# First token tile's first column group in plain float32, and weight splits spread over later slots

## The chip, the cores and the metric

One core of a Trainium2 chip runs the whole program. The metric is the device time of one execution in microseconds; the profiled times come from one execution recorded by the hardware profiler. The engines are TensorE (PE in the rows; PEld is its weight load), VectorE (DVE), ScalarE (ACT), GpSimd (POOL) and SyncE (SP), which issues most DMAs. The engines run side by side, each its own instructions strictly in program order, and wait for one another by semaphores.

## What is computed

Three float32 stages follow one another: local attention with block summaries, a dense feed-forward layer with ELU, and a routed layer of eight experts.

```python
scores = concat(masked(scale * q @ k.T, |i-j| < 16), scale * q @ k_sum.T + log(32))
x   = softmax(scores) @ concat(v, v_sum)          # (1536, 512) after the heads are joined
h   = x @ w_in                                    # 512 -> 2048
g   = where(h > 0, h, exp(min(h, 0)) - 1)         # ELU
x2  = g @ w_out                                   # 2048 -> 512
# then top-1 routing of x2 over 8 experts, relu MLP 512 -> 1024 -> 512, times the gate
```

## The kernel before

Tokens go in four tiles of 384 (`t` = 0 to 3), the 2048 hidden columns in 16 slices of 128 (`f`), which form two column groups of eight. All instructions are placed by hand in a loop over slots `sl`; in the text a slot is also named by n = sl - 9. Group 0 goes through the token tiles 0 to 3 in n = 0 to 31, group 1 in the 32 slots behind.

**Attention.** Each head pair of a tile is two units `u`, and up to slot 17 one unit belongs to a slot: scores `pe_s` into PSUM (S), `dve_max`, `act_exp`, `norm` (a 3-element TENSOR_SCALAR and a reciprocal on VectorE, then the scaling of 360 columns on GpSimd, L287), a slot later the transposes `pe_t` (T), another slot later `act_t` and the output `pe_o` (O). From slot 18 two units are worked on per pair of slots: `pe_s2`, `pe_o2` and both `norm` in the even slot, both transposes in the odd one. Slots 0 to 7 also hold `busy` transposes of the identity, whose results nobody reads.

**Split operands.** The dense layer multiplies in a reduced format (fp32r) and keeps accuracy by splitting each operand in a high part (a ScalarE cast) and a low part (a subtract). For `x` that is `act_o` and `dve_o` (VectorE); for the weights `w_split` (ScalarE L381, GpSimd L382); for the ELU result `g_hi` (ScalarE L409) and `g_lo` (GpSimd L413). Each product is then three matmuls: high x high, high x low, low x high.

**Weights** arrive as 64-bit floats. `w_load` brings a slice of 512 KB into one of four raw buffers, `w_conv` makes float32 of it in three VectorE passes (L368, L372, L375), and `w_prefetch` starts the next load. `corder` says in which slot each slice is converted, `wpend` holds the converted slices whose split is due, and `split_next` takes one of them. Between slots 17 and 32 `w_stash` converts the slices of group 1 and writes them to DRAM.

**A dense slot** (n = 0 to 7) of tile 0 runs ahead: `mm1` of slice n + 2 (12 matmuls of 384 columns into one of two PSUM banks h), ELU of slice n (`elu_exp` on ScalarE, `elu_max` on VectorE, which frees the bank), `mm2` of slice n - 1 (9 matmuls of 512 columns into three banks acc). On TensorE the order is `pe_s`, `pe_o`, `mm2`, `mm1`, `pe_t`; on VectorE `dve_max`, `elu_max`, the conversions with `dve_o` and `norm` between them. Two splits are taken per slot. Slot 8 (n = -1) is written out by hand: it holds `mm1` of slices 0 and 1, the last fourth of each behind the last `pe_o` of tile 0.

**From n = 9** a slot is: ELU of the slice before, `g_hi`, `g_lo`, a split if one is pending, `prep_k` and `prep_va` in odd slots (among them the copies L197 and L198 on VectorE), `mm2` of two slices before, in even slots `pe_o2` and `pe_s2` with their VectorE work, `mm1`, and the `w_stash` conversion. `pe_s2` uses the S bank and one h bank, so it needs that bank's `elu_max`.

Buffers: W is a pool of 16 buffers, each with the high and the low half of one slice; `xT3` is the x buffer of token tile 3, which is first written in slot 26 (n = 17).

Of the kernel before, what the change touches and what calls it, by code (L numbers as in the profile page):

```python
# [9 lines left out]
F32 = mybir.dt.float32  # L10
# [39 lines left out]
def build(tc, cap, qT, kT, vT, vP, wi, wo, wg, wgT, wx, out):  # L50
# [6 lines left out]
    with ctx:  # L57
# [79 lines left out]
        xT = {}  # L137
        acc = {}
# [172 lines left out]
        def act_o(u):  # L311
            p, t, pr, g0 = where(u)
            if pr == 0 and g0 == 0:
                xT[t] = xpool.tile([P, 2, NCC, TT], F32R, tag=f"xT{t}", name=f"xT{t}")
            nc.scalar.copy(xT[t][:, 0, pr, g0 * QB : (g0 + GRP) * QB], PS["o", u][:, 0 : GRP * QB])

        def dve_o(u):
            p, t, pr, g0 = where(u)
            q = slice(g0 * QB, (g0 + GRP) * QB)
            nc.vector.tensor_tensor(  # L320
                xT[t][:, 1, pr, q], PS.pop(("o", u))[:, 0 : GRP * QB], xT[t][:, 0, pr, q].bitcast(F32),
                op=ALU.subtract)
# [35 lines left out]

        def w_conv(which, parts=(0, 1, 2)):
            for part in parts:  # L360
                for io, f in which:
                    if part == 0:
                        raw = RW[io, f]
                        t = mpool.tile([P, 512], U32, tag="t1", bufs=T1, name=f"t1{io}{f}")
                        RW[io, f] = (raw[:, :, 0], raw[:, :, 1], t)
                    lo, hi, t = RW[io, f]
                    if part == 0:
                        nc.vector.tensor_scalar(  # L368
                            out=t, in0=hi, scalar1=3, scalar2=0x3FFFFFF8,
                            op0=ALU.logical_shift_left, op1=ALU.bitwise_and)  # L370
                    elif part == 1:
                        nc.vector.scalar_tensor_tensor(  # L372
                            out=t, in0=hi, scalar=0xC0000000, in1=t, op0=ALU.bitwise_and, op1=ALU.bitwise_or)
                    else:
                        nc.vector.scalar_tensor_tensor(  # L375
                            out=t, in0=lo, scalar=29, in1=t, op0=ALU.logical_shift_right, op1=ALU.bitwise_or)
# [10 lines left out]
        def mm1(t, f, cs=range(NCC)):  # L387
            if cs[0] == 0:
                HP[t, f] = ph(f"h{t}_{f}")
            w = W["i", f]  # L390
            for c in cs:
                for n, (s, xs) in enumerate(((0, 0), (0, 1), (1, 0))):
                    nc.tensor.matmul(  # L393
                        HP[t, f][:, 0:TT], lhsT=w[:, s, c * P : (c + 1) * P], rhs=xT[t][:, xs, c, :],
                        start=c == 0 and n == 0, stop=c == NCC - 1 and n == 2)

        def elu_exp(t, f):
            e = EP[t, f] = mpool.tile([P, TT], F32, tag="e", name=f"e{t}_{f}")
            nc.scalar.activation(out=e, in_=HP[t, f][:, 0:TT], func=AF.Exp)  # L399
            nc.scalar.activation(out=e, in_=e, func=AF.Relu, bias=1.0, scale=-1.0)  # L400
# [6 lines left out]
        def g_hi(t, f):  # L407
            gT[t, f] = mpool.tile([P, 2, TT], F32R, tag="g", name=f"g{t}_{f}")
            nc.scalar.copy(gT[t, f][:, 0], EP[t, f])  # L409

        def g_lo(t, f, eng):
            g = gT[t, f]
            eng.tensor_tensor(g[:, 1], EP.pop((t, f)), g[:, 0].bitcast(F32), op=ALU.subtract)  # L413
# [3 lines left out]
        def mm2(t, f):  # L417
            gr = f // FPG
            w = W["o", f]
            g = gT.pop((t, f))  # L420
# [3 lines left out]
            for tb in range(BPT):  # L424
                for n, (s, ws) in enumerate(((0, 0), (0, 1), (1, 0))):
# [409 lines left out]
        for f in range(NFC):  # L835
            if f < FPG:
                corder.setdefault(LAG - 4 + f, []).append(("i", f))
                corder.setdefault(LAG - 1 + f - (f > 5), []).insert(0, ("o", f))
# [5 lines left out]
        nload = [0]  # L844

# [39 lines left out]
        for sl in range(total):  # L885
# [16 lines left out]
            cv = list(corder.get(sl, ())) if sl >= LAG else []  # L902

# [13 lines left out]
            if sl == LAG - 1:  # L917
# [4 lines left out]
                w_split("i", 2)  # L922
                pe_o(u - 2)
                act_o(u - 2)
                w_conv([("o", 0)], (0, 1))
                dve_o(u - 2)
                pe_t(u - 1)
                mm1(0, 1, range(NCC - 1))
                w_conv([("o", 0)], (2,))
# [3 lines left out]
                w_split("o", 0)  # L933
                w_conv([("i", 3)], (0, 1))
                act_o(u - 1)
                dve_o(u - 1)
                mm1(0, 0, range(NCC - 1, NCC))
                mm1(0, 1, range(NCC - 1, NCC))
                w_conv([("i", 3)], (2,))
                w_prefetch()  # L940
                wpend.append(("i", 3))
# [9 lines left out]
                g_hi(0, 0)  # L951
                g_lo(0, 0, nc.gpsimd)
# [183 lines left out]
            if dense:  # L1136
# [4 lines left out]
                split_next()  # L1141
# [10 lines left out]
                wpend.extend(cv)  # L1152
# [8 lines left out]
            if sl == LAG - 3:  # L1161
                w_conv([("i", 0)], (2,))
                w_prefetch()
                w_conv([("i", 1)], (0, 1))
            if sl == LAG - 2:
                w_conv([("i", 1)], (2,))
                w_prefetch()
# [4 lines left out]
            if sl in (LAG - 3, LAG - 2):  # L1172
                w_split("i", sl - LAG + 3)
            if sl == LAG - 2:
                w_conv([("i", 2)])
                w_prefetch()
            if sl == LAG - 4:
                w_conv([("i", 0)], (0, 1))
# [289 lines left out]
```

## Time and profile before

| | |
|---|---|
| median of 3 runs | 508.42 us (508.11 to 509.48) |
| the profiled execution | 508.64 us, of which 506.9 us is the span of its instructions |
| TensorE busy | 472.0 us, 93% |
| VectorE busy | 325.6 us, 64% |
| ScalarE busy | 271.8 us, 54% |
| GpSimd busy | 189.3 us, 37% |
| mean granted TensorE clock | 0.981 |

The shares are means over stages that differ, so the rows further down are taken by stretch. In a timeline row the first number is the start in us from the span's beginning, the second the time until the last of the merged instructions ended (the pipelined matmuls of neighbouring rows overlap a little), and the bracket tells for how long the engine stood idle before it and what ended that.

### The profile page before, as it was taken

To read this page: it belongs to the slowest core of one execution; us is meant where nothing else is said; L and a number is where in the kernel's file an instruction comes from. 1 tells how busy PE (TensorE), PEld (TensorE's weight loads), DVE (VectorE), ACT (ScalarE), POOL (GpSimd) and SP (SyncE) were. 2 spreads that over 40 slices of the span, in tenths; PEclk is the share of its full clock that TensorE was granted. 3 is DMA by queue.
4 is the path that set the end of the run, shared out by engine and by line. 5 is a ranking of instruction groups with operands and counts; after the bars stand their busy time and mean duration, and the time that the engine had idled before them with its cause. 6 is when DMAs were issued, how large, how long until landed. Compare 5 with 4: busy or idle time off the path is not lost.

```text
span 506.9 us, 9236 instructions
## 1 busy us (share of the span) xinstructions
PE 472.0 (93%) x3052; PEld 406.9 (80%) x3052; DVE 325.6 (64%) x880; ACT 271.8 (54%) x681; POOL 189.3 (37%) x197
## 2 busy tenths in 40 slices
PE   7798798889999999999999999999998999999892
PEld 6586577678888889999999899888767989888672
DVE  4699999878877761111149889846686755556460
ACT  4755656666667646664333333334654865566550
POOL 4345575633333335883223233223335040030440
PEclk9988998999999999999999999999999999999997
DMA  8996656667777441439010010012645966458380
GB/s 237 283 255 185 191 162 189 214 207 245 227 230 219 126 142 46 125 118 345 37 62 2 0 63 0 2 63 88 200 129 151 345 211 222 135 164 278 105 292 15
DMA packets 45634, 79.97 MB, mean 158 GB/s; under 512 B 4604, under 2 KB 19196, under 8 KB 45552
## 3 DMA queue, kind: packets, MB, share of 16 engines
q1 hardware_dynamic: 43792, 73.83, 46.4%
q0 software_dynamic: 1760, 5.19, 3.4%
q8 instruction: 34, 0.56, 0.5%
q14 instruction: 48, 0.39, 0.2%
HBM read 65.29 MB, written 13.11 MB: 155 GB/s over the span
## 4 chain that ended last, share of the span: by engine, by line
PE 65%; DVE 15%; DMA 13%; issue 2%; ACT 2%; POOL 1%; SPq 0%; DVEq 0%; POOLq 0%
PE acc L426 23%; PE h L393 22%; DMA xgq<-x2d,gidx 10%; PE bh L750 6%; PE y L739 5%; DMA vt<-vT 2%; DVE t1i L375 2%; DVE t1i L372 2%; DVE t1o L375 1%; DMA xg<-x2d,gidx 1%; PE T L294 1%; DVE st L285 1%; DVE sc L272 1%; PE O L334 1%; DVE t1o L372 1%
## 5 line engine op out<-in xcount | busy, mean ns | idle before, releaser
L393 PE MATMUL h<-xT,Wi 128*128 128x384 f32 x768 | 152.8, 346 | 8.2 <-DVE e L404 6.6
L393 PEld LDWEIGHTS h<-xT,Wi 128*128 128x128 f32 x768 | 137.2, 192 | 16.5 <-DVE e L404 8.7
L426 PE MATMUL acc<-Wo,g 128*128 128x512 f32 x576 | 145.8, 397 | 1.0 <-POOL Wo L382 1.0
L413 POOL TENSOR_TENSOR g<-e,g 128x384 fp32r<-128x384 f32 x63 | 71.4, 1133 | 145.5 <-ACT g L409 129.9
L426 PEld LDWEIGHTS acc<-Wo,g 128*128 128x128 f32 x576 | 105.9, 188 | 21.7 <-POOL Wo L382 1.3
L404 DVE SCALAR_TENSOR_TENSOR e<-e,h 128x384 f32<-128x384 f32 x64 | 35.3, 551 | 77.3 <-ACT e L400 77.3
L399 ACT ACTIVATE e<-h 128x384 f32<-128x384 f32 x64 | 31.4, 491 | 65.4 <-PE h L393 61.8
L409 ACT CAST g<-e 128x384 fp32r<-128x384 f32 x64 | 32.8, 513 | 42.6 <-DVE e L404 42.6
L618 DVE TENSOR_TENSOR E<-rawq,E 128x512 fp32r<-128x512 f32 x70 | 46.7, 705 | 9.1 <-ACT E L608 8.0
L279 ACT ACTIVATE sc<-sc,st 128x120 f32<-128x120 f32 x96 | 36.8, 385 | 28.8 <-DVE st L272 28.6
L750 PE MATMUL bh<-xbq,E 128*128 128x256 f32 (+1 forms) x288 | 43.6, 303 | 2.7 <-ACT ysf L654 1.4
L608 ACT CAST E<-rawq 128x512 fp32r<-128x512 f32 x75 | 42.7, 617 | 6.2 <-DMA rawq<-wx 3.5
L750 PEld LDWEIGHTS bh<-xbq,E 128*128 128x128 f32 x288 | 41.3, 188 | 5.0 <-ACT ysf L654 1.6
L287 POOL TENSOR_TENSOR sc<-sc,st 128x360 f32<-128x360 f32 x32 | 29.6, 925 | 41.3 <-DVE st L286 20.1
L739 PE MATMUL y<-E,g 128*128 128x512 f32 x168 | 41.7, 393 | 0.0
L488 DVE CUSTOM_DVE_ANT_0 dot<-a,wgb 128x512 f32<-128x512 f32 x48 | 40.0, 887 | 0.0
L739 PEld LDWEIGHTS y<-E,g 128*128 128x128 f32 x168 | 30.6, 188 | 5.7
L400 ACT ACTIVATE e<-e 128x384 f32<-128x384 f32 x64 | 33.7, 526 | 2.0
L272 DVE CUSTOM_DVE_ANT_0 sc<-S,masks 128x120 f32<-128x120 f32 x96 | 21.5, 276 | 14.2 <-PE S L247 10.4
L758 DVE TENSOR_TENSOR g<-e,g 128x256 fp32r<-128x256 f32 (+1 forms) x24 | 11.3, 469 | 23.8 <-ACT g L757 23.6
L655 POOL DMA_INDIRECT out<-ys,sidx x6 | 6.3, 1053 | 47.4 <-ACT ys L654 46.0
L755 ACT ACTIVATE e<-bh 128x256 f32<-128x256 f32 (+1 forms) x24 | 10.1, 419 | 22.4 <-PE bh L750 22.4
(225 smaller groups left out, 634.5 us busy)
## 6 DMA issues: line engine op xcount, KB each, us to landing
rawq<-wx SPq DMA_DIRECT2D x88, 256.0 KB, 4.3
rawi<-wi SPq DMA_DIRECT2D x16, 512.0 KB, 5.0
rawo<-wo SPq DMA_DIRECT2D x16, 512.0 KB, 5.5
vw<-vP SPq DMA_DIRECT2D x16, 288.0 KB, 6.7
kt<-kT SPq DMA_DIRECT2D x8, 400.0 KB, 5.6
qt<-qT SPq DMA_DIRECT2D x16, 192.0 KB, 5.9
vt<-vT SPq DMA_DIRECT2D x8, 384.0 KB
out<-xg SPq DMA_DIRECT2D x12, 256.0 KB, 3.6
```

What stands on the lines that cost most here:

```text
L279: nc.scalar.activation(out=sc[:, gi], in_=sc[:, gi], func=AF.Exp, bias=st[:, 0, gi : gi + 1], scale=-1.0, accum_out=st[:, 1, gi : gi + 1])
L393: nc.tensor.matmul(HP[t, f][:, 0:TT], lhsT=w[:, s, c * P : (c + 1) * P], rhs=xT[t][:, xs, c, :], start=c == 0 and n == 0, stop=c == NCC - ...
L400: nc.scalar.activation(out=e, in_=e, func=AF.Relu, bias=1.0, scale=-1.0)
L404: nc.vector.scalar_tensor_tensor(out=e, in0=e, scalar=-1.0, in1=h[:, 0:TT], op0=ALU.mult, op1=ALU.max)
L409: nc.scalar.copy(gT[t, f][:, 0], EP[t, f])
L413: eng.tensor_tensor(g[:, 1], EP.pop((t, f)), g[:, 0].bitcast(F32), op=ALU.subtract)
L426: nc.tensor.matmul(accp[tb], lhsT=g[:, s, tb * P : (tb + 1) * P], rhs=w[:, ws], start=f % FPG == 0 and n == 0, stop=f % FPG == FPG - 1 and ...
L488: nc.vector.tensor_tensor_reduce(out=junk, in0=x2[t * BPT + tb], in1=WGB[e // 2][:, e % 2], scale=1.0, scalar=0.0, op0=ALU.mult, op1=ALU.a ...
L608: (nc.vector.tensor_copy if m in vec else nc.scalar.copy)(EW[k][m][:, 0], raw_of(k, m))
L618: (nc.gpsimd if m in pool else nc.vector).tensor_tensor(w[:, 1], raw, w[:, 0].bitcast(F32), op=ALU.subtract)
L739: nc.tensor.matmul(ys[b], lhsT=g[:, s, b * P : (b + 1) * P], rhs=w[:, ws], start=f == 0 and n == 0, stop=f == 7 and n == 2)
L750: nc.tensor.matmul(h[:, 0:nt], lhsT=EW[k][half * NCC + c][:, ws, fc * P : (fc + 1) * P], rhs=xb[:, s, c, 0:nt], start=n == 0, stop=n == 3 ...
```

## The change

For token tile 0 and the eight slices of group 0, both products are computed with plain float32 operands: the converted weights and the unsplit `x` and ELU results, one matmul instruction in place of three. The unsplit weights stand in W buffers, two slices to a buffer (the last two, slices 6 and 7 of `w_out`, in half of the buffer that token tile 3's `x` takes later); the other half of that buffer holds the unsplit `x`. `dve_o`, `g_hi` and `g_lo` are left out there. The split parts are still needed: the weights' for the other token tiles, x's for group 1. The weights are split one slice per slot in n = 1 to 16, and `x` of tile 0 in n = 11 to 14 (`split_x0`). The conversions of group 0 move one or two slots later, so that slots n = 0 to 4 convert two slices and 5 to 7 one.

```diff
         def act_o(u):
             p, t, pr, g0 = where(u)
+            if t == 0:
+                if u == 0:
+                    x = xpool.tile([P, 2, NCC * TT], F32, tag=f"xT{NT - 1}", name="x0")
+                    X0.extend([x[:, 0].rearrange("p (c q) -> p c q", q=TT), x[:, 1].bitcast(U32)])
+                nc.scalar.copy(X0[0][:, pr, g0 * QB : (g0 + GRP) * QB], PS.pop(("o", u))[:, 0 : GRP * QB])
+                return
...
+        def split_x0(c):
+            if c == 0:
+                xT[0] = xpool.tile([P, 2, NCC, TT], F32R, tag="xT0", name="xT0")
+            x = X0[0][:, c]
+            nc.scalar.copy(xT[0][:, 0, c], x)
+            nc.vector.tensor_tensor(xT[0][:, 1, c], x, xT[0][:, 0, c].bitcast(F32), op=ALU.subtract)
+
         def dve_o(u):
             p, t, pr, g0 = where(u)
+            if t == 0:
+                return
...
+        def first_weights(io, f):
+            if not T0:
+                for i, x in enumerate(splits):
+                    if i % 2 == 0 and i < 2 * FPG - 2:
+                        w = wpool.tile([P, 2, 512], U32, tag="W", name=f"T{i}")
+                    T0[x] = w[:, i % 2] if i < 2 * FPG - 2 else X0[1][:, (i % 2) * 512 : (i % 2 + 1) * 512]
+            return T0[io, f]
...
         def mm1(t, f, cs=range(NCC)):
+            if t == 0 and f < FPG:
+                for c in cs:
+                    nc.tensor.matmul(
+                        HP[t, f][:, 0:TT], lhsT=T0["i", f][:, c * P : (c + 1) * P].bitcast(F32), rhs=X0[0][:, c],
+                        start=c == 0, stop=c == NCC - 1)
+                return
...
         def mm2(t, f):
             for tb in range(BPT):
+                if whole:
+                    nc.tensor.matmul(
+                        accp[tb], lhsT=g[:, tb * P : (tb + 1) * P], rhs=w, start=f == 0, stop=f == FPG - 1)
+                    continue
...
-                corder.setdefault(LAG - 4 + f, []).append(("i", f))
-                corder.setdefault(LAG - 1 + f - (f > 5), []).insert(0, ("o", f))
+                corder.setdefault(LAG - 3 + f, []).append(("i", f))
+                corder.setdefault(LAG + f, []).insert(0, ("o", f))
...
+        splits = [("i", 0), ("i", 1)]
+        for f in range(2, FPG + 2):
+            splits += [x for x in (("i", f), ("o", f - 2)) if x[1] < FPG]
...
+            if 0 < n <= len(splits):
+                wpend.append(splits[n - 1])
+            if FPG + 3 <= n < FPG + 3 + NCC:
+                split_x0(n - FPG - 3)
...
                     g_hi(*el[1:])
                     g_lo(*el[1:], nc.gpsimd)
                 split_next()
-                split_next()
...
                 for x in cv:
                     w_prefetch()
-                wpend.extend(cv)
```

Slot 8 and the three slots ahead of it lose their four `w_split` calls, and slot 8 converts `w_in` slice 2 alone in place of two slices. `g_hi` and `g_lo` return at once for tile 0 and group 0, and the ELU result then takes a buffer of the tag g.

## Rows read from the trace of the kernel before

**Rows 1.** By stretch: length, busy us (instructions) by engine, granted clock, DMA.

```profile
46.90:88.20 41.30, 34.33 (x242) 28.06 (x241) 40.78 (x86) 23.24 (x70) 26.11 (x20) 0.92 0.60 177
119.10:130.10 11.00, 11.00 (x105) 9.60 (x101) 9.73 (x29) 6.93 (x23) 3.86 (x4) 1.00 0.85 291
```

**Rows 2.** TensorE timeline, slot n=8: start, us, engine, line, tiles, count [idle before].

```profile
97.48 0.49 PE L294 MATMUL T<-ident,sc 128*120 128x128 f32 x3
97.90 0.83 PE L258 MATMUL S<-kw,qt 64*64 64x120 f32 x12
98.70 0.57 PE L306 MATMUL O<-pT,vw 120*64 120x64 f32 x12
99.19 2.34 PE L426 MATMUL acc<-Wo,g 128*128 128x512 f32 x9
101.37 2.27 PE L393 MATMUL h<-xT,Wi 128*128 128x384 f32 x12
103.48 0.49 PE L294 MATMUL T<-ident,sc 128*120 128x128 f32 x3
```

**Rows 3.** Timeline, VectorE and GpSimd, dense slot n = 3, near 64 us.

```profile
63.69 1.24 DVE L285 TENSOR_SCALAR st<-st 128x3 f32<-128x3 f32 x1
63.18 1.72 POOL L382 TENSOR_TENSOR Wo<-t1o,Wo 128x512 fp32r<-128x512 f32 x1
```

**Rows 4.** By line: ns minimum/median/maximum of one, first and last start.

```profile
L285 DVE TENSOR_SCALAR st<-st x32: 152/157/1237, 10.4 to 178.2; 128x3 f32<-128x3 f32 x32
L382 POOL TENSOR_TENSOR Wi<-t1i,Wi x8: 1266/1295/1736, 31.2 to 81.4; 128x512 fp32r<-128x512 f32 x8
```

**Rows 5.** Timeline, TensorE: idle transposes (two, then four) and attention outputs.

```profile
22.19 0.44 PE L818 MATMUL warm<-ident 128*128 128x128 f32 x2
31.76 0.66 PE L818 MATMUL warm<-ident 128*128 128x128 f32 x4
129.21 0.92 PE L334 MATMUL O<-pT,vw 120*64 120x64 f32 x24
```

**Rows 6.** Timeline, TensorE, slot 8: its scores and its last `mm1` part.

```profile
32.67 0.83 PE L258 MATMUL S<-kw,qt 64*64 64x120 f32 x12
40.48 2.43 PE L393 MATMUL h<-xT,Wi 128*128 128x384 f32 x6 [1.62 <-ACT xT L315]
```

**Rows 7.** Timeline, slots 20 to 22: TensorE, then GpSimd, then VectorE.

```profile
119.10 0.85 PE L247 MATMUL S<-kw,qt 64*64 64x120 f32 x24
126.94 2.33 PE L426 MATMUL acc<-Wo,g 128*128 128x512 f32 x9
130.06 0.85 PE L247 MATMUL S<-kw,qt 64*64 64x120 f32 x24
124.12 1.06 POOL L287 TENSOR_TENSOR sc<-sc,st 128x360 f32<-128x360 f32 x1 [1.01 <-DVE st L286]
125.61 1.01 POOL L413 TENSOR_TENSOR g<-e,g 128x384 fp32r<-128x384 f32 x1 [0.44 <-ACT g L409]
117.95 0.55 DVE L404 SCALAR_TENSOR_TENSOR e<-e,h 128x384 f32<-128x384 f32 x1
124.44 0.55 DVE L404 SCALAR_TENSOR_TENSOR e<-e,h 128x384 f32<-128x384 f32 x1
125.77 0.97 DVE L197 COPY kw<-kt 128x192 f32<-128x192 f32 x1
129.45 0.55 DVE L404 SCALAR_TENSOR_TENSOR e<-e,h 128x384 f32<-128x384 f32 x1
```

**Rows 8.** Timeline, TensorE, slot n = 6: `mm2` and its wait.

```profile
89.46 0.49 PE L426 MATMUL acc<-Wo,g 128*128 128x512 f32 x1
90.95 2.12 PE L426 MATMUL acc<-Wo,g 128*128 128x512 f32 x8 [0.99 <-POOL Wo L382]
```

**Rows 9.** Timeline, TensorE: two `mm1` behind idle stretches.

```profile
52.45 2.35 PE L393 MATMUL h<-xT,Wi 128*128 128x384 f32 x12 [1.53 <-DVE e L404]
60.81 3.91 PE L393 MATMUL h<-xT,Wi 128*128 128x384 f32 x12 [2.11 <-DVE e L404]
```

More of the change, by code (lines that the diff above doesn't have):

```diff
@@ L137, in build @@
         xT = {}
+        X0 = []
+        T0 = {}
         acc = {}
@@ L363, in w_conv @@
                         raw = RW[io, f]
-                        t = mpool.tile([P, 512], U32, tag="t1", bufs=T1, name=f"t1{io}{f}")
+                        if f < FPG:
+                            t = first_weights(io, f)
+                        else:
+                            t = mpool.tile([P, 512], U32, tag="t1", bufs=T1, name=f"t1{io}{f}")
                         RW[io, f] = (raw[:, :, 0], raw[:, :, 1], t)
@@ L397, in elu_exp @@
         def elu_exp(t, f):
-            e = EP[t, f] = mpool.tile([P, TT], F32, tag="e", name=f"e{t}_{f}")
+            e = EP[t, f] = mpool.tile(
+                [P, TT], F32, tag="g" if t == 0 and f < FPG else "e", name=f"e{t}_{f}")
             nc.scalar.activation(out=e, in_=HP[t, f][:, 0:TT], func=AF.Exp)
@@ L407, in g_hi @@
         def g_hi(t, f):
+            if t == 0 and f < FPG:
+                return
             gT[t, f] = mpool.tile([P, 2, TT], F32R, tag="g", name=f"g{t}_{f}")
@@ L411, in g_lo @@
         def g_lo(t, f, eng):
+            if t == 0 and f < FPG:
+                return
             g = gT[t, f]
@@ L418, in mm2 @@
             gr = f // FPG
-            w = W["o", f]
-            g = gT.pop((t, f))
+            whole = t == 0 and f < FPG
+            if whole:
+                w, g = T0["o", f].bitcast(F32), EP.pop((t, f))
+            else:
+                w, g = W["o", f], gT.pop((t, f))
             if f % FPG == 0:
@@ L424, in mm2 @@
             for tb in range(BPT):
+                if whole:
+                    nc.tensor.matmul(
+                        accp[tb], lhsT=g[:, tb * P : (tb + 1) * P], rhs=w, start=f == 0, stop=f == FPG - 1)
+                    continue
                 for n, (s, ws) in enumerate(((0, 0), (0, 1), (1, 0))):
@@ L921, in build @@
                 act_t(u - 2)
-                w_split("i", 2)
                 pe_o(u - 2)
                 act_o(u - 2)
-                w_conv([("o", 0)], (0, 1))
-                dve_o(u - 2)
+                w_conv([("i", 2)], (0, 1))
                 pe_t(u - 1)
                 mm1(0, 1, range(NCC - 1))
-                w_conv([("o", 0)], (2,))
+                w_conv([("i", 2)], (2,))
                 w_prefetch()
@@ L932, in build @@
                 pe_o(u - 1)
-                w_split("o", 0)
-                w_conv([("i", 3)], (0, 1))
                 act_o(u - 1)
-                dve_o(u - 1)
                 mm1(0, 0, range(NCC - 1, NCC))
                 mm1(0, 1, range(NCC - 1, NCC))
-                w_conv([("i", 3)], (2,))
-                w_prefetch()
-                wpend.append(("i", 3))
                 fin_va(p)
@@ L950, in build @@
                 norm(u)
-                g_hi(0, 0)
-                g_lo(0, 0, nc.gpsimd)
                 continue
@@ L1160, in build @@
                     load_vt(p + 2)
[L1161 to L1167, printed above, removed]
             if sl < LAG and u - 2 in late:
@@ L1172, in build @@
             if sl in (LAG - 3, LAG - 2):
-                w_split("i", sl - LAG + 3)
-            if sl == LAG - 2:
-                w_conv([("i", 2)])
+                w_conv([("i", sl - LAG + 3)])
                 w_prefetch()
-            if sl == LAG - 4:
-                w_conv([("i", 0)], (0, 1))
             if sl >= LAG and u - 2 in late and not dense and u != NU:
```

## The prediction

> **What bounds the kernel now.** I read the busy time by stage first. In the dense slots after the first (n = 1 to 5, 46.9 to 88.2 us) VectorE is busy 40.78 of 41.30 us and TensorE only 34.33; in the pair of slots from 119.1 us it is the other way round, TensorE 11.00 of 11.00 and VectorE 9.73 [rows 1]. So the early stage runs at VectorE's pace, 41.3 / 5 = 8.26 us a slot, and from about 108 us on at TensorE's. Whatever the early stage saves reaches the end only if the stage behind it can still keep TensorE full.
>
> VectorE's 8.26 us are mostly not work. The 3-element TENSOR_SCALAR of `norm` takes 0.15 us at its shortest and 1.24 us at its longest [rows 4]. The long one began at 63.69 and ended at 64.93, just as GpSimd's weight subtract ended (63.18 + 1.72 = 64.90), and that subtract itself took 1.72 where it can take 1.27 [rows 3, 4]. The two engines block each other and take turns.
>
> The stage behind has hardly any slack. At 130.06 the score matmuls of slot 22 start as VectorE's `elu_max` ends (129.45 + 0.55 = 130.00); at 126.94 `mm2` starts 0.32 us after GpSimd's `g_lo` is done (125.61 + 1.01 = 126.62). On that path the copy of L197 already takes 0.97 us, since it waits for `g_lo` [rows 7].
>
> **Part 1: float32 matmuls.** `mm1` goes from 12 matmuls of 384 columns to 4 float32 ones, `mm2` from 9 of 512 to 3. A float32 matmul of this kernel is two records (the 6 score matmuls of a slot appear as x12) [rows 2]. None here has the whole array's shape, so I bound a record. High: two more transposes of 128 columns, whole-array float32 records, cost 0.66 - 0.44 = 0.22 us, 0.86 ns a column [rows 5]; `pe_o`'s 12 further records of 64 columns cost 0.92 - 0.57 = 0.35 us, 0.46 ns a column, or 0.91 if two of them, half the array wide each, run side by side [rows 2, 5]. So between 0.46 and 0.91 ns; I take 0.86, the row of the same shape. `mm1` is then 8 x 384 x 0.86 = 2.64 us (1.41 to 2.80) where now h to T is 103.48 - 101.37 = 2.11; `mm2` 6 x 512 x 0.86 = 2.64 where acc to h is 2.18 [rows 2]. Some 1.0 us more per slot.
>
> By the Trainium skill, FP8 and Floating Point Precision, TensorE Precision Notes, true float32 takes four passes of the array; against the three matmuls of the split this speaks against the change, and by it `mm1` would be 4/3 of 2.11 = 2.81 us, an estimate 0.2 us over mine, about 2 us over all eight slots.
>
> **Part 2: the dense stage.** A slot of TensorE is now S to O 0.80, O to acc 0.49, acc to h 2.18, h to T 2.11, T to S 0.42 [rows 2]; with part 1, 0.80 + 0.49 + 2.74 + 2.66 + 0.42 = 7.1 us. GpSimd does per slot `g_lo` (1.0 [rows 7]) and two weight subtracts (1.27 each [rows 4]) beside the softmax scale; `g_lo` and one subtract go. If VectorE waited for all of both it falls to 8.26 - 2.27 = 6.0 us a slot; if only for `g_lo`'s length, to 7.3. TensorE at 7.1 is then the bound. From the score matmuls of slot 8 (32.67) to the first `mm1` of token tile 1 (101.37) are 68.7 us [rows 2, 6]. After:
> - slot 8: the float32 halves of `mm1` (16 records, 5.3 us), S 0.8, two O 1.0, T 0.3 and a 0.5 us wait for `act_o`: 8.1 (now there is a 1.62 us wait for `act_o`, which stands on ScalarE behind weight casts that go [rows 6]);
> - n = 0: 4.2 (S, a wait for `elu_max`, `mm1`, T); n = 1: 7.4 (`mm2` waits some 0.3 for `w_out` slice 0, converted in the slot before);
> - n = 2 to 5: 4 x 7.1 = 28.4; n = 6, 7 without `mm1`: 2 x 4.65 = 9.3, though each gets a conversion;
> - n = 8 up to `mm1`: 4.35, of which `mm2` is 2.7.
>
> Sum 61.75: a gain of 6.95 us. Eight subtractions `dve_o` and the early splits go from slots 2 to 8; slots up to 7 are padded with `busy` matmuls [rows 5], so I give that nothing; without that cover it would be some 0.3 us a slot more gain. DMA issues stay two weight loads a slot on SP's queue; its cover is the four raw buffers.
>
> **Part 3: what moves behind.** Nine of the 16 splits (ScalarE cast, GpSimd subtract) now fall in n = 8 to 16, and in n = 11 to 14 `split_x0` puts a ScalarE cast and a VectorE subtract of 384 columns at the head of the slot, ahead of `elu_max`. `elu_max`, of the same 384 columns, takes VectorE 0.55 us [rows 7], neighbours overlapping a little; I take 0.5 for the subtract. Priced on the pair from 119.1 us [rows 7]:
> - `split_x0` of the odd slot stands after L375 and meets the second softmax scale, which holds GpSimd until 124.12 + 1.06 = 125.18 while `elu_max` starts at 124.44: 0.7 of wait + 0.5 = 1.2 us late;
> - the split follows `g_lo`; L197 goes first, then the subtract keeps L198 waiting: nothing if L198 won the turn, 1.27 for all of it [rows 4]; I take 1.1, since an instruction's first tenth or two overlaps its neighbour's end in these rows;
> - `split_x0` of the even slot: 0.5;
> - `norm` behind the even split: 0.1.
>
> Together 2.9 us, with 0.06 of slack. For the four pairs (scores of slots 20, 22, 24, 26): first, no `split_x0` in its odd slot, 2.0 (with 0.4 for its `norm`) less 119.10 - (117.95 + 0.55) = 0.6 of slack = 1.4; second 2.9; third, gated by `g_lo`, 1.2 + 0.1 less 0.3 of slack = 1.0. The splits also come late for their reader: `w_out` slices 5 and 7 are split in n = 14 and 16, and `mm2` of token tile 1 reads them one slot later. There a matmul starts and the next waits for GpSimd, as at 89.46 (one matmul, then 0.99 us idle) [rows 8]: VectorE's L372 takes its turn first (some 0.6, by its 0.5 for 384 columns), then the subtract, 1.7 us behind `g_lo`; `mm2` starts as `g_lo` ends and its first matmul takes 0.2, so it waits 1.5, and 1.3 where it starts 0.2 later. Sum 1.4 + 2.9 + 1.0 + 1.5 + 1.3 = 8.1 us lost (3 if the blocking hides, 10 if none does).
>
> By the Trainium skill, SBUF — State Buffer, Who interferes with whom, whichever of VectorE and GpSimd issues first has the shared ports for its whole instruction and the other is fully blocked; the 1.24 us row agrees. By it an odd split costs the whole 1.27, not 1.1, where the chain runs through it: some 0.3 us more in all.
>
> **The clock.** The granted clock is 0.92 of full speed over the dense slots and 1.00 in the pair behind [rows 1]: part of the dense stage runs at the lower level, 1.2 in place of 2.4 GHz. After TensorE had idled 1.53 us, 12 `mm1` matmuls took 2.35 us; after 2.11 us idle they took 3.91 [rows 9], and after 1.62 us six took 2.43 [rows 6]. TensorE doesn't idle in the stage behind now. In the third pair the 1.0 and 1.5 us waits lie 0.2 us apart, so I count one such fall: 3.91 - 2.35 = 1.56 (0 to 3 of them).
>
> **Sum.** The profiled run took 508.64 us (span 506.9, 1.7 around it), 0.22 above the median 508.42. 508.64 - 6.95 + 8.1 + 1.56 = 511.35; on the median's scale 511.1.
>
> **Rivals.**
> 1. *Faster: the moved splits hide.* VectorE idles 11.0 - 9.73 = 1.27 us a pair [rows 1]. If, after L197, VectorE's next port user wins the turn, the subtract slides into VectorE's idle time, and only the two late `w_out` slices cost: 508.64 - 6.95 + 2.8 = 504.5 (504.3 on the median's scale). It decides as soon as a pair's added wait stays below 1.27 us. Against it: at 64.9 both wait and they alternate. Chance 0.20.
> 2. *More clock falls*: all three long idles halve the clock: 511.35 + 2 x 1.56 = 514.5. Chance 0.17.
> 3. *VectorE stays the bound* at 8.2 in the dense slots: the gain shrinks by 5.5 us: 517. For it, the two engines' turns; against, 2.27 us of GpSimd leave. Chance 0.06.
> 4. *Float32 at the low bound*, 1.41 us: the slots fall to VectorE's 6.4, 4.5 us less: 506.9. Chance 0.07.
> 5. *It does not do what it says*: two unsplit weights share a buffer; if the halves were tracked as one, `mm1` would wait for the other half's conversion, about 3 us in five slots: 526. Against it, a matmul reads one half while GpSimd writes the other [rows 8]. Chance 0.02.
>
> **How the numbers follow.** Forecast 511.1, chance 0.48, its own range 508.5 to 513.5 (record price, turns). 0.3% is 1.5 us, about what a measurement of this kernel can tell from no change, so "same" is 506.9 to 509.9. Faster: rival 1 and half of 4, 0.23. Same: the forecast's low quarter or so and the rest of 4, 0.21. Slower: the rest, 0.56. The range, with 0.2 left out, from rival 1 to rival 2: 504.5 to 514.5.
>
> **What would show it.** Right: dense slots of about 7.1 us with TensorE nearly full; h 8 records in some 2.64 us; the first `mm1` of token tile 1 near 94.4 us; L198 and `split_x0` stretched to over 1 us in n = 10 to 14; `mm2` waiting on GpSimd in slots 24 and 26; the scores of slot 22 still 2 to 3 us ahead of 130.06, and the stage from slot 26 on that much behind its present times. Wrong: no TensorE idle between 100 and 150 us (rival 1), or dense slots still near 8.2 us with VectorE full (rival 3).

## The result and the profile after

The changed kernel took 511.92 us in the median of its first runs (509.99 to 514.62) against 508.42, a ratio of 1.0065 [1.0044, 1.0086]; in a second measurement 512.04 against 509.81, 1.0039 [1.0009, 1.0070]. The profiled execution took 511.92 us, its span 510.2. The forecast was 511.1: the total was right. Some of its parts were less so, and their misses cancel.

I cut each profile at three events: the scores of slot 8, the first `mm1` of token tile 1 (n = 8), and the scores of slot 26. The steps are from the scores of one pair to those of the next, for slots 18 to 20, 20 to 22, 22 to 24 and 24 to 26. All are differences of starts in the TensorE timelines (us), taken where the first score matmul of a pair starts. A fall is a stretch in which the granted clock is at the lower of its two levels, 1.2 in place of 2.4 GHz; the last column counts the falls between 380 us and the last ten. The rows from `x0 late` on are kernels of the experiments below.

| kernel | to slot 8 | slot 8 to `mm1` | `mm1` to slot 26 | the four steps | slot 26 to the end | falls |
|---|---|---|---|---|---|---|
| before | 32.67 | 68.70 | 50.48 | 12.69, 10.95, 10.96, 10.83 | 355.09 | 0 |
| before, again | 33.52 | 68.44 | 52.03 | 14.25, 10.95, 10.96, 10.83 | 355.12 | 0 |
| after | 32.08 | 60.59 | 60.35 | 14.24, 12.49, 16.00, 12.18 | 357.14 | 1 |
| after, again | 34.07 | 60.58 | 58.43 | 12.69, 13.60, 14.49, 12.21 | 356.81 | 1 |
| x0 late | 32.47 | 60.57 | 55.40 | 12.66, 12.12, 12.99, 12.19 | 355.57 | 0 |
| two splits a slot | 34.30 | 67.89 | 54.63 | 14.27, 11.81, 12.30, 10.83 | 357.04 | 1 |
| both | 34.24 | 66.59 | 52.28 | 14.09, 10.95, 10.96, 10.83 | 354.33 | 0 |
| x0 late, VectorE subtracts | 34.94 | 60.56 | 57.75 | 13.62, 13.50, 13.48, 11.71 | 359.73 | 2 |
| x0 late, one slot earlier | 34.57 | 61.65 | 53.14 | 12.67, 12.12, 12.07, 10.84 | 356.09 | 0 |
| x0 late, two in n = 9 | 35.53 | 60.58 | 52.69 | 12.67, 11.67, 12.07, 10.84 | 355.97 | 1 |
| the same, odd casts later | 33.06 | 60.59 | 52.68 | 12.67, 11.63, 12.10, 10.83 | 355.32 | 0 |

Before to after the spans differ by -0.59 - 8.11 + 9.87 + 2.05 = 3.2 us. So the dense stage gained 8.1 us, and all of it was given back before slot 26. The 9.87 hold two falls of the clock, at 99.67 us (`mm1` of n = 9) and at 137.22 us (`mm2` of slot 24).

By stretch (length, busy us and instructions of PE, PEld, DVE, ACT and POOL, granted clock, DMA), the four dense slots n = 2 to 5 and the pair from slot 20 read, for the changed kernel:

```profile
51.80:79.56 27.76, 27.76 (x165) 15.98 (x164) 26.56 (x68) 14.42 (x47) 11.34 (x9) 1.00 0.81 239
112.35:124.84 12.49, 11.26 (x102) 9.63 (x98) 11.43 (x30) 9.03 (x27) 6.36 (x6) 1.00 0.79 268
```

This answers [rows 1]. TensorE is now full in the dense slots, 27.76 / 4 = 6.94 us each, and at the full clock. In the pair, which took 11.00 us with TensorE full, TensorE now has holes of 1.2 us and the pair is 1.5 us longer. The TensorE timeline of slot n = 4 answers [rows 2]:

```profile
65.68 0.83 PE L260 MATMUL S<-kw,qt 64*64 64x120 f32 x12
66.44 0.57 PE L308 MATMUL O<-pT,vw 120*64 120x64 f32 x12
66.94 2.84 PE L468 MATMUL acc<-T,e 128*128 128x512 f32 x6
69.62 2.74 PE L420 MATMUL h<-x,T 128*128 128x384 f32 x8
72.20 0.49 PE L296 MATMUL T<-ident,sc 128*120 128x128 f32 x3
```

From start to start `mm2` takes 2.68 and `mm1` 2.58 us; both were put at 2.64. Behind the dense stage, slot 21 shows what the moved steps do. VectorE (with one row of an earlier slot), GpSimd, ScalarE and TensorE, each from its own timeline:

```profile
66.55 0.22 DVE L200 COPY kw<-ks 128x144 f32<-128x144 f32 x1
...
117.87 1.14 DVE L330 TENSOR_TENSOR xT<-x,xT 128x384 fp32r<-128x384 f32 x1
118.94 0.54 DVE L439 SCALAR_TENSOR_TENSOR e<-e,h 128x384 f32<-128x384 f32 x1
121.14 1.30 DVE L200 COPY kw<-ks 128x144 f32<-128x144 f32 x1
```

```profile
117.54 1.05 POOL L289 TENSOR_TENSOR sc<-sc,st 128x360 f32<-128x360 f32 x1 [1.01 <-ACT e L434]
121.05 1.30 POOL L410 TENSOR_TENSOR Wo<-T,Wo 128x512 fp32r<-128x512 f32 x1
```

```profile
119.51 0.52 ACT L446 CAST g<-e 128x384 fp32r<-128x384 f32 x1 [1.55 <-DVE e L439]
119.93 0.61 ACT L409 CAST Wo<-T 128x512 fp32r<-128x512 f32 x1
120.45 0.51 ACT L197 COPY kw<-kt 128x384 f32<-128x384 f32 x1
120.86 0.47 ACT L300 COPY pT<-T 120x384 f32<-120x384 f32 x1
```

```profile
121.47 0.52 PE L296 MATMUL T<-ident,sc 128*120 128x128 f32 x3 [1.23 <-ACT pT L300]
126.08 0.83 PE L249 MATMUL S<-kw,qt 64*64 64x120 f32 x20 [0.81 <-DVE e L439]
```

`split_x0` stands ahead of `elu_max`, meets the second softmax scale and takes 1.14 us where the `elu_max` of the same width behind it takes 0.54. `elu_max` comes late, ScalarE stood idle 1.55 us for it, and then does `g_hi`, the weight cast and the kw copy before the `pT` copy that the second transposes need: TensorE waits 1.23 us. The kw copy L200, 0.22 us where nothing is in its way, takes 1.30 beside the weight subtract; the last 20 of the 24 score records of slot 22 wait 0.81 us for the next `elu_max`. Against [rows 8], the waits for split weights are now at slots 24 and 26, where the forecast had them (the first of the two rows holds the fall at 137.22 us):

```profile
136.43 3.12 PE L472 MATMUL acc<-Wo,g 128*128 128x512 f32 x8 [0.61 <-POOL Wo L410]
150.13 2.11 PE L472 MATMUL acc<-Wo,g 128*128 128x512 f32 x8 [0.64 <-POOL Wo L410]
```

### The profile page after: what moved, and what is told of

Same layout as the page of the kernel before. It is cut to its first block, busy times and chain, and to the rows that moved or that the text cites. A ratio compares the mean times of both kernels' runs of the same rounds, so it can differ in the third digit from the quotient of the medians.

```text
span 510.2 us, 9087 instructions
## 1 busy us (share of the span) xinstructions
PE 477.8 (94%) x2996; PEld 396.7 (78%) x2996; DVE 319.3 (63%) x876; ACT 269.5 (53%) x677; POOL 179.3 (35%) x189
## 5 line engine op out<-in xcount | busy, mean ns | idle before, releaser
L427 PE MATMUL h<-xT,Wi 128*128 128x384 f32 x672 | 131.5, 342 | 0.0
L472 PE MATMUL acc<-Wo,g 128*128 128x512 f32 x504 | 128.6, 398 | 1.6 <-POOL Wo L410 1.2
L427 PEld LDWEIGHTS h<-xT,Wi 128*128 128x128 f32 x672 | 119.2, 190 | 5.9 <-issue 2.1
L472 PEld LDWEIGHTS acc<-Wo,g 128*128 128x128 f32 x504 | 93.4, 189 | 20.1 <-POOL Wo L410 1.9
L452 POOL TENSOR_TENSOR g<-e,g 128x384 fp32r<-128x384 f32 x55 | 61.5, 1119 | 128.1 <-ACT g L446 126.7
L446 ACT CAST g<-e 128x384 fp32r<-128x384 f32 x56 | 28.7, 513 | 45.0 <-DVE e L439 45.0
L300 ACT COPY pT<-T 120x384 f32<-120x384 f32 x32 | 15.3, 478 | 22.5 <-PE T L296 22.3
```

Source lines behind the costliest of these rows:

```text
L427: nc.tensor.matmul(HP[t, f][:, 0:TT], lhsT=w[:, s, c * P : (c + 1) * P], rhs=xT[t][:, xs, c, :], start=c == 0 and n == 0, stop=c == NCC - ...
L472: nc.tensor.matmul(accp[tb], lhsT=g[:, s, tb * P : (tb + 1) * P], rhs=w[:, ws], start=f % FPG == 0 and n == 0, stop=f % FPG == FPG - 1 and ...
```

## Experiments

**The change once more.** No edit.

> The changed kernel once more, nothing edited, on the same chip as the next three. Its first profile lost some 11 us between n = 9 and n = 16 and 2.4 us more behind 448 us (a longer idle before bh at 448 and a clock fall at 475). If the loss in n = 9 to 16 is systematic and the tail is drawn at random, the score matmuls of slot 26 stand again 0.9 to 1.2 us behind the kernel before, and the clock fall near 475 us is absent or elsewhere: 509.5 to 512. If the tail belongs to the change, the fall and the long idle are there again at the same instructions: 512.

512.04 us. The loss behind the dense stage is systematic: 58.43 - 50.48 = 7.95 us without any clock fall in that stretch, and slot 26 stands at 153.09 us, 1.24 behind the first profile of before. The fall near 475 us was there again.

**split_x0 in n = 23 to 26.** The unsplit x stands in the later `acc` tiles, which are free until then (the lines for that are left out here).

```diff
-            if FPG + 3 <= n < FPG + 3 + NCC:
-                split_x0(n - FPG - 3)
+            if 23 <= n < 23 + NCC:
+                split_x0((n - 23 - 1) % NCC)
```

> split_x0 moved from n = 11 to 14 to n = 23 to 26, where VectorE is idle most of the time; the unsplit x stands in the buffers of the later acc tiles. Theory (the moved steps delay elu_max and with it the pairs of score matmuls): the pairs at slots 20 to 24 no longer have a 0.5 us subtract and a 1.1 us blocked one ahead of elu_max, so slot 26 comes 3 to 5 us earlier and the run takes 507 to 509. Rival (the pairs are held by the loads of k, q and v or by the weight splits whatever stands ahead of elu_max): slot 26 moves by less than 1 us, 511 to 512.

507.94 us against 509.81, 0.9958 [0.9928, 0.9989]: a kernel 0.4% faster than before. The second and third step fall from 13.60 and 14.49 to 12.12 and 12.99; the first and last don't change. So `split_x0` cost 1.48 + 1.50 = 3.0 us. (The medians differ by 4.1; in the profiles most of the rest lies behind slot 26, 355.57 for 356.81.) The wait at T is down from 1.23 to 0.18 us, that at S to 0.36:

```profile
119.88 0.52 PE L296 MATMUL T<-ident,sc 128*120 128x128 f32 x3 [0.18 <-ACT pT L300]
124.04 0.83 PE L249 MATMUL S<-kw,qt 64*64 64x120 f32 x20 [0.36 <-DVE e L440]
```

**Two splits a slot in n = 1 to 8.**

```diff
-            if 0 < n <= len(splits):
-                wpend.append(splits[n - 1])
+            if 0 < n <= FPG:
+                wpend.extend(splits[2 * n - 2 : 2 * n])
...
                 split_next()
+                split_next()
```

> All 16 weight splits in n = 1 to 8, two a slot, none behind. Theory: TensorE's float32 matmuls bound the dense slots at 6.94 us, VectorE 6.91 busy is stretched by blocking up to that; a second subtract of 1.27 us may add up to 0.5 us a slot, 3 us over six. Behind, the waits for late w_out slices (0.6 and about 1), the blocked kw copies and half of the waits of slots 20 to 26 go, 5 us: 508 to 511. Rival A (GpSimd's turns set the dense slot, not TensorE): slots back at 8.2 us, some 1.27 us more in each of n = 1 to 7, 8 us, 514 to 516. Rival B (dense slots stay at 6.94 and everything lost behind came from the splits): 501 to 503.

512.52 us, 1.0040 [1.0008, 1.0072]. That is over the 508 to 511 of the theory and under rival A's 514 to 516. Slots n = 2 to 5 went to 7.48, 7.63, 7.49 and 7.62 us, 0.54 to 0.69 more where up to 0.5 was expected; n = 7 went from 4.84 to 9.90, since TensorE waited 2.38 us there for a converted slice and the clock fell. Of the 8.1 us of gain 0.8 is left.

**Both edits.**

> Both edits: split_x0 in n = 23 to 26 and two weight splits a slot in n = 1 to 8. Theory: nothing that was moved stands in n = 9 to 16 any more, so what the dense stage gained (8.7 us up to the first mm1 of token tile 1, less what the second subtract takes back, up to 3) reaches slot 26 and the end: 501 to 505. Rival (the stage behind gives the gain back whatever is moved into it, since loads or the order of the softmax set its pace): 508 to 511.

510.08 us, 1.0015 [0.9981, 1.0049]. The forecast of 501 to 505 failed. Half of the theory held exactly: with neither split behind the dense stage the last three steps are 10.95, 10.96 and 10.83 us, to the hundredth those of before. But the gain ahead of them was gone: VectorE, blocked by two GpSimd subtracts in a row (of its timeline in n = 5, the `norm` and a conversion pass that takes 0.66 us unblocked), falls behind, and in n = 7 TensorE waits 2.38 us for a converted slice (0.41 in after), and the clock falls, so that six matmuls take 4.54 us in place of 2.84:

```profile
82.25 1.23 DVE L287 TENSOR_SCALAR st<-st 128x3 f32<-128x3 f32 x1
83.60 1.63 DVE L404 SCALAR_TENSOR_TENSOR T<-rawo,T 128x512 uint32<-128x512 uint32 x1
```

```profile
92.49 4.54 PE L469 MATMUL acc<-wtmp,e 128*128 128x512 f32 x6 [2.38 <-DVE wtmp L404]
```

Up to `mm1` the eight splits more cost 66.59 - 60.57 = 6.0 us, 1.7 of them the fall; behind it the same eight had cost 1.17 + 2.03 + 1.36 = 4.6 us, 2.3 of them the two late slices (the run with each split one slot earlier shows that). So this move gains nothing.

**VectorE subtracts from n = 9 on** (with x0 late).

```diff
-            nc.gpsimd.tensor_tensor(w[:, 1], src, w[:, 0].bitcast(F32), op=ALU.subtract)
+            eng.tensor_tensor(w[:, 1], src, w[:, 0].bitcast(F32), op=ALU.subtract)
...
+                    w_split(*x, nc.vector if n > FPG and x in splits else nc.gpsimd)
```

> As the run with split_x0 in n = 23 to 26, and the low parts of the weight splits from n = 9 on are subtracted by VectorE in place of GpSimd. Theory (what is left of the loss behind the dense stage comes from GpSimd's subtract: it blocks VectorE's kw copies, and it is finished too late for mm2 of slices 5 and 7): a VectorE subtract of 512 columns takes some 0.7 us and blocks nobody but g_lo, so the waits of 0.65 us for Wo go and the pairs at slots 22 to 26 lose 1 to 2 us in place of 4.5: 504.5 to 506. Rival (VectorE's own length counts as much, since elu_max and the softmax steps queue behind the subtract, or g_lo is held instead): 507 to 509, the idle time before S or T grows by as much as that before acc falls.

511.60 us, 1.0029 [0.9998, 1.0059]: the theory failed, and it came out above the rival's 507 to 509 too, though the rival's mechanism is what the rows show. The waits for Wo are gone, but the steps from slot 20 to 24 are 13.5 us. VectorE's subtract first waits 1.10 us for the cast on ScalarE, in order, with the kw copies and the softmax queued behind it, and then takes 1.07, its first half beside `g_lo`; the wait at T is back at 1.20. (Its profiled execution, 514.7 us, lies above its median; its clock falls are at 26, 388 and 477 us, outside these steps.) VectorE's timeline of slot 23, then GpSimd's:

```profile
137.28 1.07 DVE L411 TENSOR_TENSOR Wo<-T,Wo 128x512 fp32r<-128x512 f32 x1 [1.10 <-ACT Wo L410]
138.27 0.25 DVE L199 COPY kw<-kt 128x192 f32<-128x192 f32 x1
```

```profile
136.80 1.00 POOL L453 TENSOR_TENSOR g<-e,g 128x384 fp32r<-128x384 f32 x1 [0.44 <-ACT g L447]
```

**Each split one slot earlier, n = 0 to 15** (with x0 late).

```diff
-            if 0 < n <= len(splits):
-                wpend.append(splits[n - 1])
+            if 0 <= n < len(splits):
+                wpend.append(splits[n])
```

> As the run with split_x0 in n = 23 to 26, and each weight split one slot earlier, so n = 0 to 15. Theory (the two waits inside mm2 in slots 24 and 26 are for w_out slices 5 and 7 split one slot ahead of their reader): both waits go, some 1.1 us each with the broken pipelining, and slot 26 comes 2 us earlier: 506. The added subtract in n = 0 costs less than 0.5, since no other split stood there. Rival (VectorE and GpSimd are full in n = 0 and the slots behind have as much to do as before): the dense stage ends up to 1.3 us later and the gain is gone: 507.5 to 508.5.

507.61 us, 0.9941 [0.9909, 0.9973]. Steps three and four fall from 12.99 and 12.19 to 12.07 and 10.84, so the two late slices had cost 0.92 + 1.35 = 2.3 us; `mm2` runs through at both places. The rival was right on the split added in n = 0, which cost 61.65 - 60.57 = 1.08 us (slot n = 1 took 8.26 in place of 7.18). TensorE at slots 24 and 26:

```profile
135.41 2.33 PE L473 MATMUL acc<-Wo,g 128*128 128x512 f32 x9
146.25 2.33 PE L473 MATMUL acc<-Wo,g 128*128 128x512 f32 x9
```

**A quarter of mm1.**

```diff
                 for c in cs:
+                    if c:
+                        continue
                     nc.tensor.matmul(
```

> The changed kernel with only the first of the four matmuls of mm1 for token tile 0 in group 0 (three quarters of that product are left out). TensorE's share of a dense slot falls by 3/4 of 2.58 = 1.9 us, to 5.0. Theory (TensorE bounds the dense slots, as the prediction has it): slots shrink from 6.94 until VectorE with GpSimd's turns is the bound, 6.0 to 6.5 us. Rival (VectorE, 6.91 busy of 6.94, bounds them already): slots stay at 6.8 to 6.95 us and TensorE idles 1.9 us in each.

Only the dense slots are read: with other x2 the tokens go to other experts, so the later stages differ (516.16 us). The four slots from n = 2 on take 25.94 / 4 = 6.49 us, VectorE is busy 25.50 of 25.94, and TensorE idles 1.34 to 1.48 us in each. So TensorE bounds the changed kernel's dense slots, and VectorE stands only 0.45 us below it. By stretch, and TensorE's wait in one of the slots:

```profile
48.93:74.87 25.94, 20.30 (x141) 11.41 (x140) 25.50 (x67) 14.55 (x49) 10.31 (x9) 1.00 0.77 240
```

```profile
64.57 2.84 PE L470 MATMUL acc<-T,e 128*128 128x512 f32 x6 [1.34 <-DVE T L403]
```

**The kernel before once more.** No edit.

> The kernel before, nothing edited, for a second profile. It tells what varies between executions of one program: if the clock fall near 475 us and the longer idle near 448 us of the changed kernel are drawn at random, they may show here too, and the early clock falls (27, 41, 61 and 78 us in the first profile) lie elsewhere; if the tail belongs to the change, the times behind 400 us repeat the first profile's within 0.3 us.

510.82 us. The stretch behind slot 26 repeats, 355.12 and 355.09. The step from slot 18 to 20 took 14.25 in place of 12.69 us: the clock fell here too, at 109.1 us, during the `mm1` of n = 9, the very place where it fell in the first profile of after (99.7 us). First after, then before again:

```profile
100.34 3.62 PE L427 MATMUL h<-xT,Wi 128*128 128x384 f32 x12
```

```profile
108.94 3.91 PE L393 MATMUL h<-xT,Wi 128*128 128x384 f32 x12
```

So this fall, 1.56 us, comes to both kernels in some executions and is not the change's. The other fall of the first profile of after, in `mm2` of slot 24, has no counterpart here: in no profile of before does the clock fall between slots 20 and 26. Both profiles of before also have falls near 61 and 78 us, in the dense stage [rows 9]; VectorE is busy 40.78 of 41.30 us there, so at most 0.5 us of them can show. After has none there.

**A second split in n = 9** (with x0 late); the splits behind it come one slot earlier.

```diff
-            if 0 < n <= len(splits):
-                wpend.append(splits[n - 1])
+            if 0 < n < len(splits):
+                wpend.extend(splits[n - 1 + (n > FPG + 1) : n + (n > FPG)])
```

> As the run with split_x0 in n = 23 to 26, with a second weight split in n = 9, so that the splits behind it come one slot earlier and end in n = 15. Theory (waits of mm2 in slots 24 and 26 are for slices split one slot ahead of their reader; n = 0 paid 1.08 us for its split, n = 9 and 10 have room): the steps from slot 18 to 26 are 12.7, 12.1, 12.1, 10.8 us as with the splits from n = 0 on, and n = 0 keeps its 7.18: slot 26 stands 4.6 us ahead of the kernel before (less what the first 32 us add), 505.5 to 507. Rival (n = 9 pays as n = 0 did): the step from slot 18 to 20 is 13.7 or more, 506.5 to 508.

505.98 us, 0.9914 [0.9885, 0.9943]. As the theory had it: n = 9 pays nothing (12.67), the dense stage keeps its 60.58, the late slices' 2.3 us stay away. The second step is even 11.67 where 12.1 was expected.

**The same, and the odd slot's split issued behind mm2.**

```diff
-                split_next()
+                if even or not attn:
+                    split_next()
                 if attn and not even and p + 1 < NPR:
                     prep_k(p + 1)
```

> As the run with a second split in n = 9, and in odd slots the split is issued behind mm2, after the kw copies, in place of ahead of them. Theory (what is left, 1.1 to 1.2 us in each of the steps from slot 20 to 22 and from 22 to 24, is the blocked kw copy on VectorE and the cast ahead of ScalarE's kw and pT copies): these two steps fall from 12.1 to 10.95 to 11.4 us, 1.4 to 2.3 us in all: 503.5 to 505.5. Rival (the loss is GpSimd's and VectorE's total work, wherever the split stands in the slot): steps stay at 11.9 to 12.2, the idle before S or T only changes its place, 506 to 507.

504.56 us, 0.9907 [0.9875, 0.9940], the lowest of all; but its steps, 11.63 and 12.10, are those of the run before, so the forecast of 10.95 to 11.4 failed. That the total fell in the 503.5 to 505.5 forecast is luck, and the interval doesn't tell it from the run before. The edit moved the cast on ScalarE and not the subtract: GpSimd starts it as soon as `g_lo` ends, beside the second kw copy as ever, and this stays blocked (1.31 us). The first kw copy takes its 0.98 us beside `g_lo`, as the kernel before has it (0.97) [rows 7]. GpSimd, then VectorE:

```profile
118.66 1.02 POOL L453 TENSOR_TENSOR g<-e,g 128x384 fp32r<-128x384 f32 x1 [0.44 <-ACT g L447]
119.64 1.30 POOL L411 TENSOR_TENSOR Wi<-T,Wi 128x512 fp32r<-128x512 f32 x1
```

```profile
118.82 0.98 DVE L199 COPY kw<-kt 128x192 f32<-128x192 f32 x1
119.72 1.31 DVE L200 COPY kw<-ks 128x144 f32<-128x144 f32 x1
```

In slot 23 both kw copies are free and a conversion pass is held instead (L404, 1.66 us for 0.69). What a subtract that meets neither would give was therefore not measured here; that the last 0.7 and 1.1 us of these steps are such blocking is argued from the rows.

**The tail: 28 more idle transposes in after, 28 fewer in before.** Slots 0 to 6 of after get two more `busy` transposes in each place; before loses 20 ahead of the first scores and 8 in slots 6 and 7.

```diff
-                busy(2 if sl < LAG - 3 else 4)
+                busy((2 if sl < LAG - 3 else 4) + 2 * (sl < LAG - 2))
```

> The changed kernel with 28 more busy transposes in slots 0 to 6, where TensorE waits anyway: TensorE then issues as many records as in the kernel before (3052; the change alone has 2996). It tells whether the 0.9 to 1.4 us idle ahead of bh near 448 us (0.5 and less before) comes from TensorE's shorter program. If it does, that idle falls to 0.5 or less and the times behind 448 us come 0.6 us earlier relative to those at 440. If it does not, it stays at 0.9 to 1.4; slot 8 moves by less than 1 us in either case, and the dense slots stay at 6.94.

> The kernel before with 28 fewer busy transposes (20 of the 24 ahead of the first scores, 2 of 4 in each place of slots 6 and 7), so TensorE issues 2996 records as in the changed kernel. With 28 more of them the changed kernel idled 2.96 us ahead of bh near 448 us and lost 8 us behind 440 us. Theory (the idle ahead of the first bh behind a branch depends on how long TensorE's program is, not on what the change computes): here it is 0.9 to 1.4 us as in the changed kernels, where the kernel before has 0.5 or less, and the times behind 448 us shift by 0.6 to 0.9 us against those at 440; the median is 1 to 2.5 us over the kernel before: 510 to 512.5. Rival (the tail's idle comes from something else that the change moved): idle 0.5 or less, shift behind 448 us within 0.3, median within 1 us of the kernel before.

515.83 us, 1.0114 [1.0068, 1.0160], and 513.11 us, 1.0086 [1.0050, 1.0122]. The counts in the two expectations were wrong: such a transpose leaves one record, so both kernels come to 3024, between after's 2996 and before's 3052. Up to slot 26 neither moved: 60.59 and 60.36 us for the two stages of the padded kernel (60.59 and 60.35 in after), 68.69 and 52.01 for the shortened one (68.44 and 52.03 in before again). Behind slot 26 they took 362.31 and 358.80 us, 5.2 and 3.7 more than after and before again. Much of it is lost ahead of a row near 448 us, the first `bh` (the first product of an expert) behind a branch; before, after, padded, shortened:

```profile
446.55 4.58 PE L750 MATMUL bh<-xbq,E 128*128 128x256 f32 x36 [0.50 <-issue]
```

```profile
448.10 4.58 PE L796 MATMUL bh<-xbq,E 128*128 128x256 f32 x36 [1.17 <-issue]
```

```profile
449.13 6.07 PE L796 MATMUL bh<-xbq,E 128*128 128x256 f32 x36 [2.96 <-issue]
```

```profile
451.89 4.58 PE L750 MATMUL bh<-xbq,E 128*128 128x256 f32 x36 [2.56 <-issue]
```

With 3052 records the idle is 0.50 us and, in the second profile, none; with 2996, 0.89 to 1.40 in nine profiles; with 3024, 2.56 and 2.96. So it goes by the length of TensorE's program ahead of it, in either kernel, though not in proportion.

The packets of the instruction queues in the traces show by what. In all thirteen profiles (the quarter run, with its other experts, left out) the last packet of 16 KB on queue q8 landed 1.38 to 1.52 us before this `bh` started. In the first profile of before it was sent at 444.20 us, 1.85 us before TensorE fell idle; in the padded kernel at 446.17, just when TensorE fell idle, and it landed at 447.74. So TensorE waits there for its next instructions; how the length sets when they come is not shown beyond the three lengths. The padded kernel has a second such wait, inside the next expert, 1.50 us behind the landing of another such packet:

```profile
478.69 6.76 PE L722 MATMUL bh<-E,xbq 128*128 128x512 f32 x17 [2.55 <-issue]
```

Of the padded kernel's 5.2 us some 1.8 are the first wait, 1.7 the idle time at the next expert, 1.5 a fall of the clock at 450 us. In the shortened one 2.5 are the wait; the rest is not taken apart here.

## Why the prediction came out as it did

**Part 1, right.** 2.58 and 2.68 us against 2.64: the row of the same shape, the transposes, was the one to price by. By the four passes of the Trainium skill, FP8 and Floating Point Precision, TensorE Precision Notes, `mm1` was estimated at 2.81, 0.23 over the trace. The measured factor is 2.58 / 2.11 = 1.22 and not 4/3. (0.17 us over the prediction's own 2.64 is 1.4 us over eight slots, not 2.)

**Part 2, right in kind, 1.2 us too small.** 60.59 us against 61.75. Slots n = 2 to 5 took 6.94 and not 7.1 (0.6 in all): the sum had entered 2.74 and 2.66 for the two products where part 1 had 2.64 for each, and they took 2.68 and 2.58. The stretch of n = 8 up to `mm1` took 3.8 and not 4.35. (Slot 8's terms add up to 7.9, where 8.1 was entered; it took 8.28.) TensorE is the bound, as stated, with VectorE at 6.5, inside the 6.0 to 7.3 given. That VectorE's 8.26 us were "mostly not work" went too far: with `g_lo` and one subtract gone it still needs the 6.5. Rivals 3, 4 and 5 fall: the slots are neither at VectorE's 8.2, nor at its 6.4, nor longer for a shared buffer. What the step doesn't say, and two splits a slot showed, is how near VectorE stands.

**Part 3, 8.1 forecast, 7.95 measured** (58.43 - 50.48), and the sizes were right pair by pair. Up to the scores of slots 20, 22, 24 and 26, 1.4, 2.9, 2.5 and 1.3 us were forecast. The second profile, cut at the first score record as in the table, gives 0.4, 2.6, 3.5 and 1.4. But that cut puts 1.1 us into the wrong pair: at slots 20 and 22 of this profile four records run ahead and the other 20 wait for `elu_max`, where in before all 24 go together. At slot 20:

```profile
112.79 0.42 PE L249 MATMUL S<-kw,qt 64*64 64x120 f32 x4
114.06 0.83 PE L249 MATMUL S<-kw,qt 64*64 64x120 f32 x20 [0.85 <-DVE e L439]
```

Cut at the first of those 20 in both kernels, the pairs lose 1.5, 2.6, 2.4 and 1.4 us. In the third pair the sum came out and its parts did not: it was to be "gated by `g_lo`", 1.0, with 1.5 of wait for the split weights behind it. The wait that counts runs through ScalarE, where the late `elu_max` holds `g_hi`, the weight cast, the kw copy and then the `pT` copy (1.23 us at T, in slot 23 as in slot 21), a path the prediction didn't look at: `mm2` of slot 24 started 9.26 us behind the 20 score records of slot 22 in place of 7.69, so 1.6 late, and its wait for the split weights cost 0.9 more. By cause, of the 7.95: `split_x0` 3.0, the late slices 2.3, the other splits 1.17 + 1.11 = 2.3 (12.12 - 10.95 and 12.07 - 10.96), and 0.4 around the first `mm1`. That the 2.3 belong to splits is shown by the run with both edits, whose steps are those of before; that it is the subtract's blocking is argued from the rows. Rival 1, all hidden but 2.8, falls; of rival 2's three falls in this stretch the first profile has two, the second none.

**The clock, right in price and place, a term too large.** One fall of 1.56 us was counted, in the third pair. The first profile of after has it there, behind waits of 1.24 us at T and 0.61 for the split weights (the step takes 16.00 us in place of 14.49), and so has the padded kernel (16.02), which is the same in this stretch. The second profile and the quarter run (14.49), again the same there, don't, and no profile of before does. In two of four executions it is worth some 0.8 us on average, not 1.56. The other fall of the first profile, in `mm1` of n = 9, belongs in no sum for the change, since before has it in some executions too.

**What was missing: the tail.** The two profiles of after take 2.05 and 1.7 us longer behind slot 26 than those of before, where no instruction was changed. The wait ahead of `bh` (1.17 and 1.08 us for 0.50 and none) and a clock fall near 475 us are in both. The runs with 28 transposes and the instruction packets show that this is a wait for instructions and that the length of the program changes it. The fall is in five of the nine profiles with 2996 records, so it may be a matter of the execution. Without falls in the stretches ahead, the stages that the change touches come out even, -8.11 + 7.95 = -0.2 us; with the tail's 1.7 to 2.05 and the 0.8 of the third pair's fall that makes 2.3 to 2.7 us, an estimate from few profiles. The medians differ by 2.2 and 3.5; that nothing else is in them is not shown.

So the total was right by luck: 1.2 us of gain too few, and 0.8 us of fall too many, stood in for a tail of about 2 us.

By the Trainium skill, Runtime: NRT & Kernel Launch, Instruction fetch mechanics, instructions are fetched ahead in sequence, and a taken branch to a place that isn't at hand stops the engine until that block is fetched. The trace agrees so far: `bh` follows the branch on an expert's count of tokens, the idle's releaser is "issue", and it ends 1.38 to 1.52 us behind an instruction packet. No run here moved the branch alone.

By the Trainium skill, SBUF — State Buffer, Who interferes with whom, the engine that issues second on the shared ports is blocked for the other's whole instruction. L200's 1.30 us beside a subtract of 1.30, and the 1.14 us of `split_x0`, agree.

## What to carry to other kernels

Work that is moved out of a full stage is priced at the place it goes to, and there by who stands behind it on its engine: the moved splits cost 3.0 us (x) and 4.6 us (weights) in the slots chosen, and moving `split_x0` by twelve slots and seven of the weight splits by one made of a loss of 0.4 to 0.65% a gain of 0.9%. Moving the steps to where VectorE idles did this; moving them back into the full stage, or to another engine with the same queue behind it, did not. Cut both traces at a few common events before reading waits: it separates what a change did from what an execution drew. Take events that wait for the same thing in both: the first score record of a pair, which runs ahead of the rest, put 1.1 us into the wrong step.

## What was unexpected of the hardware

- TensorE's idle ahead of the first matmul behind a branch was 0 to 0.5 us, 0.9 to 1.4 us, or 2.6 to 3.0 us in programs of 3052, 2996 and 3024 TensorE records, with the work between unchanged; 28 transposes that nobody reads, 400 us earlier, moved a run by 4 us. In each profile the idle ended 1.38 to 1.52 us after a 16 KB packet of instructions had landed.
- One and the same place, the `mm1` of n = 9, keeps the full clock in some executions and loses 1.56 us in others, in both kernels. The `mm2` of slot 24 does so behind the same waits in two of four executions of the changed schedule.
